# Fill-in products on TensorE in the early stage, a plan with other DMA costs, and query exponentials in two steps

## The chip, the cores and the metric

The kernel runs as one program on one core of a Trainium2 chip. A core has five engines, each with an instruction queue of its own that is worked off strictly in order: TensorE (PE in the profile, its weight loads PEld), VectorE (DVE), ScalarE (ACT), GpSimd (POOL) and SyncE (SP), which here only issues DMAs. The metric is the time of one execution in microseconds of the device; the median of three runs is given. The profile is one further execution with the hardware profiler on.

## The reference

Inputs are q, k and v of shape (8 batches, 8 heads, 576 rows, 64), three gate matrices of 512 x 768 and an output matrix of 768 x 512, the weights handed in as float64 and taken apart by the kernel.

```python
q_s = exp(q - max(q, axis=-1)); q_s /= sum(q_s, axis=-1) + 1e-9      # per row of q
k_s = exp(k - max(k, axis=2));  k_s /= sum(k_s, axis=2) + 1e-9       # per column of k, over the rows
kv = einsum('bhsd,bhse->bhde', k_s, v)
x = einsum('bhsd,bhde->bhse', q_s, kv)  -> (4608 rows, 512)
h = max(x @ w1, x @ w2, x @ w3)
out = h @ w_out
```

## The kernel before, in words

**Work.** A batch has four pairs of heads; pair n = 4b + g gives 128 of the 512 columns of x for the 576 rows of batch b. The second half of the program takes x in chunks of 512 rows (chunk c is the first 512 rows of batch c; the 64 left over from each batch make a ninth chunk). A chunk needs 18 gate products (6 column blocks j by 3 matrices), each a sum over the four pairs cc and over three matmuls per pair (high and low halves of x and w in fp32r), and then a second layer of 4 row blocks t by 6 blocks j by 3 matmuls. Each weight block (a *slice*, 24 in all: 18 of the gates, 6 of the output matrix) is loaded as float64 bits and turned into a high and a low fp32r part by ACT, DVE and POOL (`Slice.join`, `low_word`, `hi`, `lo`).

**A pair of the first two batches** (`turned`) goes through these TensorE steps: keys are transposed (`k_turned`, lines 419 and 423), their maxima taken by DVE (428 to 430), exponentials by ACT (434, 435), transposed back (442, 444), copied out (451), multiplied with v (`k_steps`, 489), scaled into a block matrix (505). The queries are shifted, exponentiated and normed (`q_steps`), transposed (`turned_steps`, 612 and 616), copied out (621, 623) and multiplied with the block matrix (`x_steps`, 639); lines 642 and 644 split the result into the two halves of x. Pairs in the list `Q_BY_ACT` have their query exponentials done as ten small ACT instructions with the row sum in each (543); the others have a subtraction on DVE or POOL (548), one ACT exponential (563) and a DVE sum (565).

**Order.** The order of all instructions on all engines is written by a planner (`Streams`) while the program is built. Each stream is a generator of `Step`s with an engine (or a choice of two), a cost in microseconds, what it waits for, which buffers ("rooms") it takes and frees, and a rank. The planner keeps a clock for each engine (S, A, V, G, T for SP, ACT, DVE, POOL, PE), lets the step begin that can begin first, and takes among those that can begin together the one of lowest rank; ranks come from due times (`AT` for the pairs of the first two batches, `FIRST + CHUNK * (b - 1)` for later batches, `SLICES_AT + SLICE * n` for slices, `GATES_AT` for gates). Instructions are emitted in the order in which the plan begins their steps, and the chip then runs each engine's queue in that order, with semaphores where data or memory demand it. The plan's costs thus decide the order only.

**Small products.** One tile named `ps` of four quarters of 128 columns (line 283) holds the small TensorE results: line 423's and 444's last transposes, 616's, the kv product of 489 and the 64-row product of 639. They take the quarters in turn (`small`, line 284). Larger results go to `pa` (attention) and `pf` (gates and second layer).

**First loads.** SP issues the loads of batch 0 and the first six slices in the order of the string `FIRST_LOADS` (a small letter is one pair's 512 rows or one slice w, a capital the 64 left-over rows). Three slices can be staged at a time (`ROOMS`).

Of the kernel before, what the change touches and what calls it, by code (L numbers as in the profile page):

```python
# [25 lines left out]
SIGNAL = 0.22  # L26
AHEAD = 0.5
DMA_LANDS = 2.0
DMA_RATE = 300.0
WAIT = 0.02  # L30

FIRST, CHUNK, SLICE = 27.0, 66.0, 2.7

AT = (7.3, 14.2, 18.2, 22.2, 39.0, 46.0, 63.0, 66.0)
STEP = (1.4, 2.8)
SLICES_AT, SLICE_STEP, SLICE_HI, SLICE_LO = 11.4, 0.18, 1.23, 1.56
GATES_AT = 50.0
FIRST_LOADS = 'kKqQvVwkqKQwvVkqwvkqvw'
ROOMS = 3, 2, 3, 4

Q_BY_ACT = (0, 1, 2, 3, 5, 6, 7)


def dve(n):
# [33 lines left out]
class Streams:  # L78
# [3 lines left out]
    def __init__(self, rooms, queued):  # L82
        self.all, self.when = [], {}
        self.queued = queued
        self.rooms = rooms
        self.taken = {}
        self.freed = {}
        self.clock = dict.fromkeys("SAVGT-", 0.0)
        self.port = 0.0
        self.queues = 0.0  # L90

# [3 lines left out]
    def ready(self, s, engine):  # L95
# [24 lines left out]
            t = max(t, self.port)  # L120
        return t

    def advance(self, s, engine=None):
        try:
            s[4] = s[0].send(engine)
        except StopIteration:
            self.all.remove(s)
# [25 lines left out]

    def issue(self, t, e, c, s):
        step = s[4]
        end = t + c
        self.clock[e] = end
        if e in step.port:
            self.port = end
        if step.kb:  # L160
            self.queues = max(self.queues, end) + step.kb / DMA_RATE
            end = self.queues + DMA_LANDS
        s[3], s[5] = end, e
        if step.gives:
            self.when[step.gives] = end
        for r, key in step.take:
            self.taken.setdefault(r, []).append(key)
        for f in step.free:
            self.freed[f] = end
        s[1] += s[2]  # L170
        self.advance(s, e)
# [3 lines left out]
def linear_attention_then_maxout_ffn(  # L175
# [26 lines left out]
    nc = tc.nc  # L202
# [75 lines left out]
    in_pf = []  # L278
    for c in range(B + 1):
        in_pf += [(c, j, i) for j in range(NJ) for i in range(3)] + [(c, "y", t) for t in range(4)]  # L280
    st = Streams({"pf": 4, "pa": 3, "ps": 4, "keT": 1, "hp": NJ, "tmp": 3, "ke": 2, "qe": 2, "qf": 1, "qt": 2, "tb": 1, "qT": 2, "qhl": 1}, {"pf": in_pf})
    late_pools, turn_pools = [], []
    quarters = ps.tile([P, 4, P], F32, name="ps")
    small = (quarters[:, i % 4, :] for i in itertools.count())

# [64 lines left out]
    class Pair:  # L352
# [19 lines left out]
        def k_load(self):  # L372
            if self.b:
                prev = self.ago("ksub") if self.n >= NP + 2 else None
                if self.turned:
                    yield Step("S", 1.1, [prev], kb=256)
                    for hh in range(2):
                        nc.sync.dma_start(out=self.kt[:, 0:4, hh, :], in_=head_rows(k, self.b, 2 * self.g + hh))
                else:
                    yield Step("S", 0.55, [prev], kb=256)  # L380
                    nc.sync.dma_start(out=self.kt[:, :, 0:4, :], in_=main_rows(k, self.b, self.hs))
                yield Step("S", 0.5, gives=("k", self.n), kb=32)
                nc.sync.dma_start(
                    out=self.kt[0:LEFT, 4] if self.turned else self.kt[0:LEFT, :, 4, :], in_=left_rows(k, self.b, self.hs)
                )

        def v_load(self):
            if self.b:
                prev = self.ago("kv") if self.n >= NP + 2 else None
                for hh in range(2):  # L390
                    yield Step("S", 0.6, [prev], kb=128)
                    nc.sync.dma_start(out=self.vt[:, hh, 0:4, 0:D], in_=head_rows(v, self.b, 2 * self.g + hh))
                yield Step("S", 0.5, gives=("v", self.n), kb=32)
                nc.sync.dma_start(out=self.vt[0:LEFT, :, 4, 0:D], in_=left_rows(v, self.b, self.hs))

        def q_load(self):
            if self.b == 0:
                return
            if self.turned:
                prev = self.ago("qsub") if self.n >= NP + 2 else None  # L400
                self.qt = qbuf[self.m]
                yield Step("S", 0.55, [prev], kb=256)
                nc.sync.dma_start(out=self.qt[:, :, 0:4, :], in_=main_rows(q, self.b, self.hs))
                yield Step("S", 0.5, gives=("q", self.n), kb=32)
                nc.sync.dma_start(out=self.qt[0:LEFT, :, 4, :], in_=left_rows(q, self.b, self.hs))
            else:
                yield Step("S", 0.55, ["turn"], gives=("q", self.n), take=[("qt", self.n)], kb=288)
                self.qt = turn_pools[0].tile([P, QS, D], F32, name="qt", bufs=2)
                nc.sync.dma_start(out=self.qt, in_=q[self.b, self.hs].rearrange("h (p s) d -> (h p) s d", s=QS))

# [108 lines left out]
        def q_steps(self):  # L519
# [6 lines left out]
            if self.turned:  # L526
# [2 lines left out]
                    out=qm.rearrange("p (h s) -> p h s", h=2), in_=src, op=ALU.max, axis=AX.X, negate=by_act  # L529
                )  # L530
                if by_act:
                    yield Step("A", rows * 0.33, take=[("qe", n)], gives=("qsub", n))
                else:
                    e = yield Step(
                        "VG", (dve(rows * D), pool(rows * D)), take=[("qe", n)], gives=("qsub", n), port="VG"
                    )
# [2 lines left out]
                sums = qs.rearrange("p (s h) -> p s h", h=2)  # L539
                if by_act:  # L540
                    for hh in range(2):
                        for s in range(5):
                            nc.scalar.activation(  # L543
                                out=qe[:, s, hh, :], in_=src[:, hh, s, :], func=AF.Exp,
                                bias=qm[:, 5 * hh + s : 5 * hh + s + 1], accum_out=sums[:, s, hh : hh + 1],
                            )
                else:
                    unit[e].tensor_tensor(
                        out=qe.rearrange("p s h d -> p h s d"),
                        in0=src,  # L550
                        in1=qm.rearrange("p (h s) -> p h s", h=2).unsqueeze(3).broadcast_to([P, 2, 5, D]),
                        op=ALU.subtract,
                    )
# [7 lines left out]
            if not by_act:  # L561
# [1 line left out]
                nc.scalar.activation(out=rows3, in_=rows3, func=AF.Exp)  # L563
                yield Step("V", dve_reduce(rows * D))
                nc.vector.tensor_reduce(out=qs, in_=rows3, op=ALU.add, axis=AX.X)
            yield Step("V", 0.28)
            nc.vector.tensor_scalar_add(out=qs, in0=qs, scalar1=1e-9)
            nc.vector.reciprocal(out=qs, in_=qs)
            which, cost = ("VG", (dve(rows * D), pool(rows * D))) if self.turned else ("V", dve(rows * D))
# [78 lines left out]
    class Chunk:  # L648
# [47 lines left out]
        def second(self, t):  # L696
# [14 lines left out]
            o = tmp.tile([P, DM], F32, name="m")  # L711
            nc.scalar.copy(out=o, in_=po)  # L712
            if c < B:
                yield Step("S", 0.5, kb=256, free=[("tmp", (c, "y", t))], rank=-1000.0)
                rows = out[c * S : c * S + CH, :]
                if c < TURNED:
                    nc.sync.dma_start(out=rows.rearrange("(p s) d -> s p d", s=4)[t], in_=o)
                else:
                    nc.sync.dma_start(out=rows[ts, :], in_=o)
            else:  # L720
                for i in range(2):
                    yield Step("S", 0.5, kb=128, free=[("tmp", (c, "y", t))] if i else (), rank=-1000.0)
                    end = (2 * t + i + 1) * S
                    nc.sync.dma_start(out=out[end - LEFT : end, :], in_=o[i * LEFT : (i + 1) * LEFT, :])

# [9 lines left out]
    def first_loads():  # L735
# [3 lines left out]
        for ch in FIRST_LOADS:  # L739
            g = seen.get(ch, 0)  # L740
            seen[ch] = g + 1
            hs = slice(2 * g, 2 * g + 2)
            low = ch.lower()
            if ch == "w":
                yield Step("S", 0.6, gives=("wst", g), kb=512, take=[("wst", g)])
                slices[g].load(start, N_ST, N_X)
            elif ch == "k":
                yield Step("S", 1.1, gives=("kmain", g), kb=256)
                for h in (2 * g, 2 * g + 1):
                    nc.sync.dma_start(out=k0[:, 0:4, h, :], in_=head_rows(k, 0, h))  # L750
            elif ch in to:
                yield Step("S", 0.55, gives=("%smain" % ch, g), kb=256)
                nc.sync.dma_start(out=to[ch][:, hs, 0:4, :], in_=main_rows(of[ch], 0, hs))
            else:
                hs = slice(2, H) if g else slice(0, 2)
                yield Step("S", 0.6, gives=(ch, g), kb=32 if g == 0 else 96)
                nc.sync.dma_start(out=to[low][0:LEFT, hs, 4, :], in_=left_rows(of[low], 0, hs))  # L757

    def landed(g):
# [32 lines left out]
        st.add(f(), 0.0)  # L792

    def slice_load(sl, late):
        yield Step("S", 0.55, ["late"] if late else (), gives=("wst", sl.n), take=[("wst2" if late else "wst", sl.n)], kb=512)
        sl.load(late_pools[0] if late else start, N_ST2 if late else N_ST, N_X2 if late else N_X)

    def slice_done(sl, late):
# [80 lines left out]
```

## Time and profile before

| what | value |
|---|---|
| median of three runs | 721.54 us (720.34 to 723.81) |
| the profiled execution, its own time | 724.52 us |
| its span, first to last instruction | 722.4 us |
| TensorE busy | 690.8 us, 96% of the span |
| VectorE busy | 404.8 us, 56% |
| ScalarE busy | 256.5 us, 36% |
| GpSimd busy | 58.4 us, 8% |
| mean granted TensorE clock | 0.993 |
| moved by DMA | 58.07 MB |

The busy time of TensorE is that of pipelined matmuls: a matmul is listed with its whole latency, and the next one begins before it has ended, so the spacing of starts and not the listed duration says how fast a group went. The chain of waits is free of this: it gives to each piece only the time that passed before the next. The shares of busy time are means over the span; the first 130 us look different from the rest, and the stages are read one by one below.

### The profile page before, as it was taken

The numbers are of one execution on the slowest core, as the hardware profiler recorded it, in microseconds if no ns is written. First come the engines' busy times: TensorE is split into PE (matmuls) and PEld (weight loads), VectorE is DVE, ScalarE is ACT, GpSimd is POOL, SyncE is SP. The second block draws the span as 40 slices with busy tenths as digits, with TensorE's granted clock in tenths as the row PEclk, the third lists the DMA queues.
The fourth block names the chain that finished last, engine by engine and source line by source line (L and its number), as shares of the span: only waits on it lengthen the run. The fifth ranks groups of instructions, "written<-read, shape, count | busy, mean of one in ns | idle before, by whom it ended". The sixth has DMA issues, their size and how long they took to land.

```text
span 722.4 us, 9841 instructions
## 1 busy us (share of the span) xinstructions
PE 690.8 (96%) x3528; PEld 553.5 (77%) x3528; DVE 404.8 (56%) x806; ACT 256.5 (36%) x610; POOL 58.4 (8%) x68
## 2 busy tenths in 40 slices
PE   3789999899999999999999999999999999999997
PEld 2557777677787887788878887888888888888886
DVE  6779997689988985675467646723222102211220
ACT  5878886333344324322342234212311111111111
POOL 2222432201000000000001000000000000000000
PEclk9989999999999999999999999999999999999999
DMA  7938414443445412530154005300100010000002
GB/s 212 257 110 252 134 61 135 141 104 99 110 125 155 113 46 69 143 109 1 33 146 126 18 25 149 83 1 10 66 1 0 15 44 0 1 33 26 1 0 59
DMA packets 86417, 58.07 MB, mean 80 GB/s; under 512 B 53344, under 2 KB 77920, under 8 KB 86368
## 3 DMA queue, kind: packets, MB, share of 16 engines
q1 hardware_dynamic: 86368, 57.44, 28.1%
q8 instruction: 28, 0.46, 0.3%
q14 instruction: 21, 0.17, 0.1%
HBM read 40.89 MB, written 9.44 MB: 70 GB/s over the span
## 4 chain that ended last, share of the span: by engine, by line
PE 85%; DVE 6%; DMA 3%; ACT 2%; SPq 2%; issue 1%; POOL 0%; DVEq 0%; ACTq 0%
PE pf L669 60%; PE pf L707 18%; PE ps L489 3%; PE pa L639 3%; ACT qe L543 1%; DMA kt<-in_k_dram 1%; PE ps L639 1%; DMA wst<-in_moe_w_dram 1%; SPq L589 1%; DVE ke L467 1%; PE pa L612 0%; DVE x L644 0%; DVE tb L576 0%; DMA qt<-in_q_dram 0%; SPq L757 0%
## 5 line engine op out<-in xcount | busy, mean ns | idle before, releaser
L669 PE MATMUL pf<-x,wh 128*128 128x512 f32 x1152 | 361.1, 395 | 1.1 <-DVE x L644 1.1
L669 PEld LDWEIGHTS pf<-x,wh 128*128 128x128 f32 x1152 | 218.0, 189 | 50.5 <-DVE x L644 1.7
L669 PE MATMUL pf<-x,wl 128*128 128x512 f32 x576 | 232.1, 403 | 0.9 <-ACT x L642 0.9
L681 DVE TENSOR_TENSOR m<-pf,m 128x512 f32<-128x512 f32 x108 | 74.3, 688 | 185.6 <-PE pf L669 185.0
L669 PEld LDWEIGHTS pf<-x,wl 128*128 128x128 f32 x576 | 109.2, 190 | 26.7 <-ACT x L642 1.1
L684 ACT CAST h_h<-m 128x512 fp32r<-128x512 f32 x54 | 33.5, 621 | 208.0 <-DVE m L681 208.0
L707 PE MATMUL pf<-ol,h_h 128*128 128x512 f32 x216 | 89.1, 412 | 0.0
L707 PE MATMUL pf<-oh,h_l 128*128 128x512 f32 x216 | 84.6, 392 | 0.0
L707 PE MATMUL pf<-oh,h_h 128*128 128x512 f32 x216 | 84.3, 390 | 0.0
L678 ACT COPY m<-pf 128x512 f32<-128x512 f32 x54 | 31.6, 586 | 52.2 <-PE pf L669 51.9
L687 DVE TENSOR_TENSOR h_l<-m,h_h 128x512 fp32r<-128x512 f32 x54 | 38.0, 704 | 20.7 <-ACT h_h L684 20.6
L707 PEld LDWEIGHTS pf<-ol,h_h 128*128 128x128 f32 x216 | 40.6, 188 | 9.0 <-issue 0.5
L707 PEld LDWEIGHTS pf<-oh,h_l 128*128 128x128 f32 x216 | 40.5, 188 | 8.9
L707 PEld LDWEIGHTS pf<-oh,h_h 128*128 128x128 f32 x216 | 40.7, 188 | 7.6 <-issue 0.5
L464 POOL PARTITION_ALL_REDUCE kma<-km x24 | 20.0, 832 | 305.3 <-DVE km L461 166.5
L669 PE MATMUL pf<-left,wh 128*128 128x512 f32 x144 | 44.3, 389 | 0.0
L712 ACT COPY m<-pf 128x512 f32<-128x512 f32 x36 | 21.1, 586 | 62.2 <-PE pf L707 61.3
L333 POOL TENSOR_TENSOR wst<-wx,wst 128x512 int32<-128x512 int32 x24 | 33.6, 1400 | 89.2 <-DVE wx L329 38.9
L576 DVE STREAM_TRANSPOSE tb<-qt 128x576 f32<-128x576 f32 x24 | 30.5, 1271 | 11.3 <-DMA qT<-tb 10.7
L669 PEld LDWEIGHTS pf<-left,wh 128*128 128x128 f32 x144 | 27.0, 188 | 5.6
L489 PEld LDWEIGHTS ps<-vt,ke 128*64 128x64 f32 (+1 forms) x560 | 18.9, 137 | 14.8 <-issue 5.0
L563 ACT ACTIVATE qt<-qt 128x576 f32<-128x576 f32 x24 | 16.5, 688 | 36.9 <-DVE qt L558 36.8
(110 smaller groups left out, 690.3 us busy)
## 6 DMA issues: line engine op xcount, KB each, us to landing
wst<-in_moe_w_dram SPq DMA_DIRECT2D x18, 512.0 KB, 4.2
out_dram<-m SPq DMA_DIRECT2D x32, 256.0 KB, 2.2
vt<-in_v_dram SPq DMA_DIRECT2D x56, 128.0 KB, 3.0
qt<-in_q_dram SPq DMA_DIRECT2D x24, 288.0 KB, 3.1
qT<-tb SPq DMA_DIRECT2D x192, 36.0 KB, 1.9
kt<-in_k_dram SPq DMA_DIRECT2D x24, 256.0 KB, 3.1
wst<-in_moe_w_out_dram SPq DMA_DIRECT2D x6, 512.0 KB, 3.3
q<-in_q_dram SPq DMA_DIRECT2D x8, 256.0 KB, 4.6
```

The lines of the kernel that those rows point to most:

```text
L333: nc.gpsimd.tensor_add(out=low.bitcast(I32), in0=x.bitcast(I32), in1=low.bitcast(I32))
L464: nc.gpsimd.partition_all_reduce(kma, km, P, bass_isa.ReduceOp.max)
L489: nc.tensor.matmul(out=kv[r, :nv], lhsT=ke[rows, s, hh, :], rhs=self.vt[rows, hh, s, 0:nv], start=(s == 0), stop=(s == 4),)
L576: nc.vector.transpose(out=tb.rearrange("p e (c s) -> p s e c", s=QS), in_=self.qt.rearrange("p s (e c) -> p s e c", e=2))
L639: nc.tensor.matmul(out=xT, lhsT=l, rhs=r[:, cs], start=(i == 0), stop=(i == last))
L669: nc.tensor.matmul(out=ps, lhsT=l[:, cc, js], rhs=r, start=(cc == 0 and t == 0), stop=(cc == NC - 1 and t == 2))
L678: nc.scalar.copy(out=m, in_=self.m.pop((j, 0)))
L681: nc.vector.tensor_max(out=m, in0=self.m.pop((j, i)), in1=m)
L684: nc.scalar.copy(out=h, in_=m)
L687: unit[e].tensor_sub(out=lo, in0=m, in1=h.bitcast(F32))
L707: nc.tensor.matmul(out=po, lhsT=l, rhs=r[:, j, :], start=(j == 0 and i == 0), stop=(j == NJ - 1 and i == 2))
L712: nc.scalar.copy(out=o, in_=po)
```

## The change

Five things are changed.

- **Fill-in products.** Before the planner emits a TensorE step it looks how long its clock for TensorE has stood. Where that is over 0.3 us and the plan's time is between 4.2 and 70 us, it first emits `int((idle - 0.3) / 0.22) + 1` products of the 128 x 128 identity with itself. Their result goes to the fourth quarter of `ps` and is never read. The plan's own clocks do not count them.
- **Small products get three quarters** in place of four, in the program and in the plan (`"ps": 3`).
- **Query exponentials.** The ten ACT instructions of line 543 are planned as two steps of five, so that the planner can put other ACT work between them; pairs 2 and 3 leave `Q_BY_ACT` and take the other way.
- **Costs of the plan.** DMA steps cost 0.64 us on SP (1.28 for two) in place of 0.5 to 0.6 (1.1), the data rate is 356 KB per us, and 0.62 of that for transfers begun before 16 us, in place of 300 throughout; loads in short rows count as larger (400 for 256 KB); the engines' clocks begin at 0.72 to 4 us and not at 0.
- **Due times** of pairs, slices and later batches are other numbers, and two of the last first loads change places.

No instruction of the computation is added or taken away except by the way that pairs 2 and 3 go.

```diff
-DMA_RATE = 300.0
+DMA_RATE, DMA_FIRST, DMA_AT_FIRST = 356.0, 0.62, 16.0
-FIRST, CHUNK, SLICE = 27.0, 66.0, 2.7
-AT = (7.3, 14.2, 18.2, 22.2, 39.0, 46.0, 63.0, 66.0)
-STEP = (1.4, 2.8)
-SLICES_AT, SLICE_STEP, SLICE_HI, SLICE_LO = 11.4, 0.18, 1.23, 1.56
+WARM_FROM, WARM_TO, WARM_IDLE, WARM_COST = 4.2, 70.0, 0.3, 0.22
+FIRST, CHUNK, SLICE = 22.7, 71.1, 2.7
+AT = (7.3, 14.2, 20.3, 22.2, 41.7, 48.7, 66.4, 62.3)
+STEP = (0.7, 3.92)
+SLICES_AT, SLICE_STEP, SLICE_HI, SLICE_LO = 11.4, 0.29, 1.44, 1.56
-FIRST_LOADS = 'kKqQvVwkqKQwvVkqwvkqvw'
+FIRST_LOADS = 'kKqQvVwkqKQwvVkqwqkvvw'
-Q_BY_ACT = (0, 1, 2, 3, 5, 6, 7)
+Q_BY_ACT = (0, 1, 5, 6, 7)
...
-        self.clock = dict.fromkeys("SAVGT-", 0.0)
+        self.clock = {"S": 0.72, "A": 2.2, "V": 4.0, "G": 3.0, "T": 0.0, "-": 0.0}
...
+    def keep_warm(self, t):
+        idle = t - max(self.clock["T"], WARM_FROM)
+        if t < WARM_TO and idle > WARM_IDLE:
+            self.fill(int((idle - WARM_IDLE) / WARM_COST) + 1)
...
     def issue(self, t, e, c, s):
         step = s[4]
+        if e == "T":
+            self.keep_warm(t)
         end = t + c
...
-            self.queues = max(self.queues, end) + step.kb / DMA_RATE
+            begun = max(self.queues, end)
+            self.queues = begun + step.kb / DMA_RATE / (DMA_FIRST if begun < DMA_AT_FIRST else 1.0)
...
-    st = Streams({"pf": 4, "pa": 3, "ps": 4, "keT": 1, "hp": NJ, "tmp": 3, "ke": 2, "qe": 2, "qf": 1, "qt": 2, "tb": 1, "qT": 2, "qhl": 1}, {"pf": in_pf})
+    st = Streams({"pf": 4, "pa": 3, "ps": 3, "keT": 1, "hp": NJ, "tmp": 3, "ke": 2, "qe": 2, "qf": 1, "qt": 2, "tb": 1, "qT": 2, "qhl": 1}, {"pf": in_pf})
+    def fill(n):
+        for _ in range(n):
+            nc.tensor.matmul(out=idle, lhsT=ident, rhs=ident, start=True, stop=True)
+    st.fill = fill
     quarters = ps.tile([P, 4, P], F32, name="ps")
-    small = (quarters[:, i % 4, :] for i in itertools.count())
+    small = (quarters[:, i % 3, :] for i in itertools.count())
+    idle = quarters[:, 3, :]
...
                 if by_act:
-                    yield Step("A", rows * 0.33, take=[("qe", n)], gives=("qsub", n))
+                    yield Step("A", 5 * 0.33, take=[("qe", n)])
...
                     for hh in range(2):
+                        if hh:
+                            yield Step("A", 5 * 0.33, gives=("qsub", n))
```

More of the change, by code (lines that the diff above doesn't have):

```diff
@@ L375, in k_load @@
                 if self.turned:
-                    yield Step("S", 1.1, [prev], kb=256)
+                    yield Step("S", 1.28, [prev], kb=400)
                     for hh in range(2):
@@ L379, in k_load @@
                 else:
-                    yield Step("S", 0.55, [prev], kb=256)
+                    yield Step("S", 0.64, [prev], kb=256)
                     nc.sync.dma_start(out=self.kt[:, :, 0:4, :], in_=main_rows(k, self.b, self.hs))
-                yield Step("S", 0.5, gives=("k", self.n), kb=32)
+                yield Step("S", 0.64, gives=("k", self.n), kb=50)
                 nc.sync.dma_start(
@@ L390, in v_load @@
                 for hh in range(2):
-                    yield Step("S", 0.6, [prev], kb=128)
+                    yield Step("S", 0.64, [prev], kb=200)
                     nc.sync.dma_start(out=self.vt[:, hh, 0:4, 0:D], in_=head_rows(v, self.b, 2 * self.g + hh))
-                yield Step("S", 0.5, gives=("v", self.n), kb=32)
+                yield Step("S", 0.64, gives=("v", self.n), kb=50)
                 nc.sync.dma_start(out=self.vt[0:LEFT, :, 4, 0:D], in_=left_rows(v, self.b, self.hs))
@@ L401, in q_load @@
                 self.qt = qbuf[self.m]
-                yield Step("S", 0.55, [prev], kb=256)
+                yield Step("S", 0.64, [prev], kb=256)
                 nc.sync.dma_start(out=self.qt[:, :, 0:4, :], in_=main_rows(q, self.b, self.hs))
-                yield Step("S", 0.5, gives=("q", self.n), kb=32)
+                yield Step("S", 0.64, gives=("q", self.n), kb=50)
                 nc.sync.dma_start(out=self.qt[0:LEFT, :, 4, :], in_=left_rows(q, self.b, self.hs))
             else:
-                yield Step("S", 0.55, ["turn"], gives=("q", self.n), take=[("qt", self.n)], kb=288)
+                yield Step("S", 0.64, ["turn"], gives=("q", self.n), take=[("qt", self.n)], kb=288)
                 self.qt = turn_pools[0].tile([P, QS, D], F32, name="qt", bufs=2)
@@ L565, in q_steps @@
                 nc.vector.tensor_reduce(out=qs, in_=rows3, op=ALU.add, axis=AX.X)
-            yield Step("V", 0.28)
+            yield Step("V", 0.34)
             nc.vector.tensor_scalar_add(out=qs, in0=qs, scalar1=1e-9)
@@ L713, in second @@
             if c < B:
-                yield Step("S", 0.5, kb=256, free=[("tmp", (c, "y", t))], rank=-1000.0)
+                yield Step("S", 0.64, kb=256, free=[("tmp", (c, "y", t))], rank=-1000.0)
                 rows = out[c * S : c * S + CH, :]
@@ L721, in second @@
                 for i in range(2):
-                    yield Step("S", 0.5, kb=128, free=[("tmp", (c, "y", t))] if i else (), rank=-1000.0)
+                    yield Step("S", 0.64, kb=128, free=[("tmp", (c, "y", t))] if i else (), rank=-1000.0)
                     end = (2 * t + i + 1) * S
@@ L744, in first_loads @@
             if ch == "w":
-                yield Step("S", 0.6, gives=("wst", g), kb=512, take=[("wst", g)])
+                yield Step("S", 0.64, gives=("wst", g), kb=512, take=[("wst", g)])
                 slices[g].load(start, N_ST, N_X)
             elif ch == "k":
-                yield Step("S", 1.1, gives=("kmain", g), kb=256)
+                yield Step("S", 1.28, gives=("kmain", g), kb=400)
                 for h in (2 * g, 2 * g + 1):
@@ L751, in first_loads @@
             elif ch in to:
-                yield Step("S", 0.55, gives=("%smain" % ch, g), kb=256)
+                yield Step("S", 0.64, gives=("%smain" % ch, g), kb=256)
                 nc.sync.dma_start(out=to[ch][:, hs, 0:4, :], in_=main_rows(of[ch], 0, hs))
@@ L755, in first_loads @@
                 hs = slice(2, H) if g else slice(0, 2)
-                yield Step("S", 0.6, gives=(ch, g), kb=32 if g == 0 else 96)
+                yield Step("S", 0.64, gives=(ch, g), kb=50 if g == 0 else 150)
                 nc.sync.dma_start(out=to[low][0:LEFT, hs, 4, :], in_=left_rows(of[low], 0, hs))
@@ L794, in slice_load @@
     def slice_load(sl, late):
-        yield Step("S", 0.55, ["late"] if late else (), gives=("wst", sl.n), take=[("wst2" if late else "wst", sl.n)], kb=512)
+        yield Step("S", 0.64, ["late"] if late else (), gives=("wst", sl.n), take=[("wst2" if late else "wst", sl.n)], kb=512)
         sl.load(late_pools[0] if late else start, N_ST2 if late else N_ST, N_X2 if late else N_X)
```

## The prediction

> **What bounds the kernel now.** I read first the page's slices of the span and the busy times by stage, then the chain of waits, then who VectorE and TensorE waited for before 62.8 us. In the page's slices (tenths of busy time, and the clock) the first two of forty show a TensorE with much idle time; in the stage rows the columns are the stretch, its length, busy us and instructions of PE, PEld, DVE, ACT and POOL, the granted clock, DMA share and GB/s.
>
> ```profile
> PE   3789999899999999999999999999999999999997
> PEclk9989999999999999999999999999999999999999
> ```
>
> ```profile
> 4.00:33.40 29.40, 17.76 (x89) 12.62 (x90) 20.16 (x48) 20.68 (x93) 6.39 (x5) 1.00 0.98 262
> ...
> 37.10:44.00 6.90, 6.02 (x32) 4.13 (x32) 5.20 (x14) 4.21 (x12) 1.29 (x1) 0.51 0.34 101
> 44.00:62.70 18.70, 16.07 (x109) 10.91 (x109) 16.71 (x36) 16.41 (x55) 5.92 (x4) 1.00 0.58 156
> 62.70:133.00 70.30, 70.25 (x362) 55.43 (x363) 59.92 (x117) 51.80 (x136) 22.20 (x22) 1.00 0.42 137
> 133.00:146.20 13.20, 9.77 (x68) 7.31 (x67) 9.86 (x20) 4.43 (x9) 1.42 (x2) 0.88 0.55 158
> ```
>
> From 62.7 to 133 us TensorE never stands (70.25 of 70.30). So an early gain counts only as far as TensorE gets more of its fixed work done before 62.7, and as VectorE keeps up behind. The clock rows say 0.51 for 37.1 to 44 and 1.00 for 4 to 33.4, but the second is not to be trusted, as the chain of waits shows (start, time until the next piece, what):
>
> ```profile
> 22.93 3.43 ACT qe L543 x20
> ...
> 28.54 1.46 PE ps L489 x20
> 30.00 2.86 PE pf L669 x6
> ...
> 37.98 1.54 PE ps L489 x20
> 39.52 2.00 PE pa L639 x2
> 41.52 1.28 PE pf L669 x3
> ...
> 43.12 0.85 PE pa L612 x4
> ...
> 62.76 19.08 PE pf L669 x83
> 81.84 0.88 PE ps L489 x20
> ...
> 87.81 0.86 PE pa L639 x2
> ...
> 95.07 0.44 PE pa L612 x4
> ```
>
> The same twenty instructions of line 489 take 1.46 us at 28.5, 1.54 at 38.0 and 0.88 at 81.8; line 639's two take 2.00 and 0.86, line 612's four 0.85 and 0.44. So TensorE ran at about half speed at 28 us too, where the clock row shows 1.00. The chain holds six cold pieces: 1.46 + 2.86 + 1.54 + 2.00 + 1.28 + 0.85 = 9.99 us. Warm they cost 0.88 + 1.38 + 0.88 + 0.86 + 0.69 + 0.44 = 5.13 (a gate matmul is 19.08 / 83 = 0.23). The half clock thus costs **4.9 us** on this chain.
>
> The other engines feel it as waits. VectorE between 5 and 46 us waited for (us in total, times, longest):
>
> ```profile
> DVE left L644 <- PE ps L444: 2.5, 1, 2.5
> ...
> DVE left L644 <- ACT left L642: 1.5, 1, 1.5
> DVE ke L451 <- ACT qe L543: 1.3, 1, 1.3
> DVE ke L451 <- PE ps L423: 0.9, 1, 0.9
> DVE qs L567 <- ACT qe L543: 0.7, 1, 0.7
> DVE km L429 <- PE ps L489: 0.4, 1, 0.4
> ```
>
> VectorE matters as much as TensorE, because the second layer of the first chunk ends with the last weight slice:
>
> ```profile
> 128.06 0.68 DVE L348 TENSOR_TENSOR ol<-wst,oh 128x512 fp32r<-128x512 f32 x1
> ```
>
> ```profile
> 133.02 0.40 PE L669 MATMUL pf<-x,wl 128*128 128x512 f32 x1
> ```
>
> The slice is split at 128.74; four row blocks of three matmuls still need it, 12 x 0.23 = 2.8 us, so the next chunk's gates could begin at 131.5 and do begin at 133.0. VectorE has only 1.5 us to spare: a gain above that must come from VectorE getting through its work sooner.
>
> **The change, part by part.** The sum is made against the profiled execution: 724.5 us, of which 722.4 are span; it lies 3.0 above the median of the runs, 721.5, to which I apply the difference.
>
> *Fill-in products and the clock.* If TensorE is at full speed from about 10 us on, TensorE's 4.9 us go, and with them VectorE's waits that hang on cold products: 2.5 + 1.5 + 0.9 + 0.4 = **-5.3** (the 1.5 is line 642, itself behind a cold product). I take VectorE's figure, since its work has the last word at 131.5. If the clock stays low it is 0.
>
> [...]
>
> How many products: TensorE idles 11.6, 0.9 and 2.6 us in the three early stage rows, 15.1 us; the plan reckons warm, so half of the 17.76 + 6.02 busy us is idle time to it as well, at most 27.0 together. At 0.22 that makes 69 to 123 products, an estimate. One costs a quarter of line 639's 512 columns: 0.86 / 4 = 0.22 warm, twice that cold.
>
> *What the products delay.* They wait for nothing of their own, but stand ahead of the next useful product. By the diff's costs the plan has the first keys at 6.26 and the first transposes at 6.98, so 12 products stand before them: 12 x 0.43 = 5.2 us at half speed, from 4.2 to 9.4, where the transposes now begin at 4.47:
>
> ```profile
> 4.47 1.08 PE L419 MATMUL pa<-ident,k 128*128 128x128 f32 x4 [4.47 <-DMA k<-in_k_dram]
> ...
> 11.37 1.12 PE L442 MATMUL pa<-ident,keT 128*128 128x128 f32 x4 [5.51 <-ACT keT L434]
> ...
> 17.00 1.53 PE L489 MATMUL ps<-v,ke 128*64 128x64 f32 x20 [0.92 <-DVE km L429]
> ```
>
> ```profile
> 7.96 0.16 DVE L430 TENSOR_TENSOR km<-km 128x1 f32<-128x1 f32 x1
> ...
> 16.73 0.21 DVE L429 TENSOR_REDUCE km<-ps 128x1 f32<-128x64 f32 x1
> ```
>
> ```profile
> 10.56 0.66 ACT L434 ACTIVATE keT<-pa,km 128x512 f32<-128x512 f32 x1
> ```
>
> The maxima are ready at 8.12 and ACT takes them at 10.56, 2.4 us later, so of the 4.9 us of delay 2.5 come through. The next idle time, 5.51 us before line 442, is filled as well, and there is a catch. Line 489's product at 17.00 goes into the first quarter of `ps`, and it was released by line 429 at 16.94, which reads the third: the quarters share one memory, and writes of TensorE wait for reads of any quarter that were emitted ahead. Products put before line 442 thus wait for line 435's read and run behind it, up to 5.5 us more for pair 0. Together 0 to 8.0; below nothing is excluded, since added products release nothing. I take a fifth, **+1.6**: four or five pairs are under way before x is complete at 62.7, and pair 0, the first of them, has its 5.51 and 2.4 us of slack in work of others that ACT and VectorE do meanwhile.
>
> *Query exponentials.* Pairs 2 and 3 leave ACT, where a pair took 3.43 us on the chain, for this way (from the row of pair 4, which goes it already):
>
> ```profile
> 56.41 0.82 DVE L548 TENSOR_TENSOR qe<-q,qm 128x640 f32<-128x640 f32 x1
> ...
> 61.29 0.81 DVE L565 TENSOR_REDUCE qs<-qe 128x10 f32<-128x640 f32 x1
> ```
>
> ```profile
> 58.42 0.74 ACT L563 ACTIVATE qe<-qe 128x640 f32<-128x640 f32 x1
> ```
>
> ```profile
> L322 DVE TENSOR_SCALAR wx<-wst 128x512 uint32<-128x512 uint32 x7 | 2.9, 413 | 2.6 <-DMA wst<-in_moe_w_dram 2.6
> ```
>
> VectorE gains work, 2 x (0.82 + 0.81) = 3.3 us (1.6 if both subtractions go to POOL), and loses the waits on line 543, 1.3 + 0.7 = 2.0. ACT is freed of 2 x (3.43 - 0.74) = 5.4 us and can take back slices' line 322, which the plan gives to either engine: four of the seven, 1.7 us, is my choice between none and 2.9. Net 3.3 - 2.0 - 1.7 = **-0.4**, from -3.3 (POOL takes the subtractions, ACT all seven) to +3.3 (nothing saved). The step split in two adds no instruction.
>
> *Three quarters, other costs, other due times.* Three quarters can make a product wait that finds a free one now. The waits of TensorE before 62.8:
>
> ```profile
> PE pa L442 <- ACT keT L434: 9.0, 2, 5.5
> ...
> PE ps L489 <- ACT qf L623: 2.8, 1, 2.8
> PE ps L489 <- DVE km L429: 1.1, 2, 0.9
> ```
>
> The 2.8 is a product that found its quarter taken, so the price of a fourth less is 0 to another 2.8; since any read of `ps` holds up TensorE already, I take 0. The new order of loads and due times is bounded by what is left of VectorE's idle time, the same rows: from -2.0 to +2.0, taken as 0, hidden behind the 70.25 busy us of TensorE. That cover is gone if a slice comes over 1.5 us late.
>
> **Sum:** -5.3 + 1.6 - 0.4 = -4.1: the profiled execution would be 720.4, the median 721.5 - 4.1 = **717.4 us**. Half a per cent, 3.6 us, is about what a measurement of this kernel can tell from no change.
>
> **The rivals.**
>
> *The products stand behind reads (slower).* Of TensorE's waits above, 9.0 + 2.8 + 1.1 = 12.9 us end with an engine that reads `ps`. If each is followed by products of its own length, the clock's gain is eaten: -5.7 for clock and exponentials, +2.5 for the first block, plus a share of 12.9. From a quarter of it on (3.2) the change is slower than before; at three quarters it is +6.5, 728.0. For it: line 489 released by line 429 above. Against it: most of the 9.0 lies before 23 us, where other pairs' work is at hand.
>
> [...]
>
> *Nothing comes through.* x is complete earlier, but slice 23 is not, because VectorE's 3.3 us of new work and the late start (1.6) eat the waits saved; or the clock does not stay up because TensorE still stands while products wait for reads, and the change does not do what it says. -5.3 - 2.0 + 3.3 + 1.6 = -2.4 with nothing taken over by ACT, +1.6 with no clock gain and the exponentials even; about 721.
>
> *More than the sum.* The stage from 133 to 146.2 loses 13.2 - 9.77 = 3.4 us of TensorE's time, and at clock 0.88 another 1.2. It hangs on the order in which the first pairs of batch 2 come; a new order may close it: 717.4 - 4.6 = 712.8.
>
> **How the numbers follow.** Forecast 0.36 (own range 714 to 719, five parts in six of it faster by over 3.6), nothing comes through 0.28 (719 to 723), products behind reads 0.22 (above 725), more than the sum 0.14 (below 714). Faster: 0.30 + 0.14 = 0.44; within half a per cent: 0.06 + 0.28 = 0.34; slower: 0.22. From 711 to 726 some 0.17 is left out, half of the slow case and half of the best one.
>
> **What would show it.** Right: line 489's twenty instructions take 0.9 us from the second pair on; line 419 begins near 9 us; VectorE's waits on line 444 and on line 642 are gone; x's last line 644 ends some us before 62.7, and the last split of `ol` before 126. The slow rival shows as groups of identity products that begin right at the end of lines 429, 435, 451 or 623, with the useful product behind them. The second shows as an early x with the last split of `ol` still near 128. The prediction is wrong if TensorE's transposes still take 0.85 us after 15 us, or if TensorE stands for long after 62 us.

## The result

| kernel | median us | ratio to the kernel before, same chip (95% interval) |
|---|---|---|
| before | 722.35 | |
| changed | 743.12 | 1.0291 (1.027 to 1.0312) |

The change makes the kernel 2.9% slower, some 20.8 us. The profiled execution went from 724.52 to 742.59 us, its span from 722.4 to 740.8. That lies outside the range of the prediction.

### The profile page after: what moved, and what is told of

The parts are those of the page before. It is cut to its first block, busy times and chain, and to the rows that moved or that the text cites. A ratio compares the mean times of both kernels' runs of the same rounds, so it can differ in the third digit from the quotient of the medians.

```text
span 740.8 us, 10184 instructions
## 1 busy us (share of the span) xinstructions
PE 707.8 (96%) x3708; PEld 573.1 (77%) x3708; DVE 403.4 (54%) x801; ACT 253.7 (34%) x574; POOL 65.0 (9%) x75
## 4 chain that ended last, share of the span: by engine, by line
PE 85%; DVE 4%; issue 4%; ACT 2%; SPq 2%; DMA 1%; POOL 1%; ACTq 0%; DVEq 0%; POOLq 0%
PE pf L689 53%; PE pf L727 20%; PE ps L297 4%; PE pa L659 3%; PE ps L507 3%; SPq L609 1%; PE ps L659 1%; DMA kt<-in_k_dram 1%; DVE tb L596 1%; PE pa L632 0%; ACT qe L563 0%; PE pa L460 0%; POOL kma L482 0%; DVE m L701 0%; POOL h_l L707 0%
## 5 line engine op out<-in xcount | busy, mean ns | idle before, releaser
L707 DVE TENSOR_TENSOR h_l<-m,h_h 128x512 fp32r<-128x512 f32 x48 | 33.7, 702 | 20.6 <-ACT h_h L704 20.6
L297 PE MATMUL ps<-ident 128*128 128x128 f32 x180 | 26.6, 303 | 18.0 <-ACT keT L453 4.5
L482 POOL PARTITION_ALL_REDUCE kma<-km x24 | 17.7, 738 | 280.2 <-DVE km L479 140.8
L297 PEld LDWEIGHTS ps<-ident 128*128 128x128 f32 x180 | 23.6, 209 | 21.0 <-ACT keT L453 5.6
L485 DVE TENSOR_TENSOR ke<-kt,kma 128x640 f32<-128x640 f32 x24 | 19.5, 814 | 24.8 <-POOL kma L482 24.8
```

The costliest lines, as they stand in the source:

```text
L297: nc.tensor.matmul(out=idle, lhsT=ident, rhs=ident, start=True, stop=True)
L707: unit[e].tensor_sub(out=lo, in0=m, in1=h.bitcast(F32))
```

## The profile after

The first of the page's slices shows a TensorE that is busier than before (6 tenths for 3), the second does not (6 for 7):

```profile
PE   6688999989999999999999799999999999999997
...
PEclk9989999999999999999999999999999999999999
```

The stage rows (columns as in the prediction) are cut at 75.2, 148 and 160 us where those of before are cut at 62.7, 133 and 146.2: TensorE is steadily busy from 75.5 us on, not from 62.8.

```profile
4.00:30.00 26.00, 20.01 (x162) 18.32 (x163) 11.15 (x26) 12.91 (x57) 5.03 (x4) 1.00 0.96 264
30.00:75.20 45.20, 36.95 (x250) 28.27 (x249) 32.08 (x77) 28.23 (x82) 8.57 (x7) 0.89 0.36 103
75.20:148.00 72.80, 71.26 (x369) 55.83 (x368) 61.41 (x119) 51.79 (x135) 23.51 (x22) 1.00 0.43 135
148.00:160.00 12.00, 9.40 (x67) 7.16 (x66) 7.02 (x15) 4.92 (x9) 1.42 (x2) 0.86 0.47 143
160.00:740.80 580.80, 570.23 (x2868) 463.57 (x2864) 288.90 (x552) 154.34 (x289) 24.31 (x28) 1.00 0.22 60
```

VectorE and ACT tell the story of the first row: they work 11.15 and 12.91 of the first 26 us, where before they were busy 20.16 and 20.68 of 29.4. TensorE's busy time is largely that of the products. In the chain of waits they are pieces of their own (start, us, what):

```profile
4.01 4.31 PE ps L297 x24
8.31 0.45 PE pa L437 x4
...
11.03 3.17 PE ps L297 x26
14.20 0.45 PE pa L460 x4
...
15.61 1.83 PE ps L297 x14
17.44 0.90 PE ps L507 x20
...
37.90 2.56 PE pf L689 x6
40.46 0.78 PE pa L632 x4
...
72.88 2.05 PE ps L297 x16
...
75.47 24.52 PE pf L689 x108
```

At first the clock does what was hoped for: line 437's four transposes take 0.45 us at 8.3 us (0.85 for such a group at 43 before) and line 507's twenty instructions 0.90 at 17.4 (1.46 at 28.5 before). It does not stay up: six gate products of line 689 take 2.56 us at 37.9, where six took 1.38 at full speed before, and the granted clock of the stretch from 30 to 40 us is 0.71. And 3.17 us of products stand between the end of what line 460 waited for and line 460. The page's group of the products, and who TensorE waited for before 100 us:

```profile
L297 PE MATMUL ps<-ident 128*128 128x128 f32 x180 | 26.6, 303 | 18.0 <-ACT keT L453 4.5 <-DVE ident L268 4.0 <-ACT qf L643 2.5
```

```profile
PE ps L297 <- ACT keT L453: 4.5, 2, 2.5
PE ps L297 <- DVE ident L268: 4.0, 1, 4.0
PE ps L297 <- ACT qf L643: 2.5, 3, 1.5
PE ps L297 <- DVE left L664: 2.1, 2, 1.5
PE ps L297 <- ACT ke L469: 2.1, 1, 2.1
PE ps L297 <- DVE km L447: 1.1, 2, 0.7
PE ps L297 <- DVE ke L469: 0.9, 1, 0.9
PE ps L297 <- ACT bdf L523: 0.8, 1, 0.8
```

There are 180 instructions, two to a product, so 90 products, 26.6 us. Of the 18.0 us of waiting in front of them, 4.0 are for the identity itself; the other 14.0 are all for engines that read `ps` (lines 453, 643, 664, 469, 447, 523). The products read nothing but the identity and write a quarter that nobody reads; still they waited for reads of the other quarters, 14.0 us in all, and then ran in full in front of the product that the read had made ready. It goes the other way too: line 523, which reads the keys' product out of `ps`, waited twice, 2.8 us in all, for products that stood behind that one:

```profile
ACT bdf L523 <- PE ps L297: 2.8, 2, 2.2
```

The last split of batch 0's 512 rows of x, and the last split of the output weights (the low part `ol` of the last slice):

```profile
71.08 0.68 DVE L664 TENSOR_TENSOR x<-pa,x 128x512 fp32r<-128x512 f32 x1
```

```profile
144.55 0.68 DVE L366 TENSOR_TENSOR ol<-wst,oh 128x512 fp32r<-128x512 f32 x1
```

Below, x is called complete when these 512 rows are: at 71.8 us here, 62.7 before. The steady stage of TensorE begins at 75.5 for 62.8 us, 12.7 later, and the last split comes at 144.55 for 128.06, 16.5 later. A third loss lies far behind all this. From 160 us on TensorE idles 580.8 - 570.2 = 10.6 us (7.0 in the answering stage before), most of it at one place, which the instructions of POOL and TensorE show:

```profile
412.49 1.61 POOL L707 TENSOR_TENSOR h_l<-m,h_h 128x512 fp32r<-128x512 f32 x1 [7.09 <-DVE qm L576]
420.39 0.72 POOL L482 PARTITION_ALL_REDUCE kma<-km  x1 [6.30 <-issue]
```

```profile
423.74 0.80 PE L689 MATMUL pf<-x,wl 128*128 128x512 f32 x1 [5.46 <-DVE m L701]
```

The new plan gives 6 of the 54 low halves of the hidden layer (`h_l`, line 707) to POOL, where VectorE did all 54 before. The five all-reduces that come right after one begin 5.9 to 6.3 us after its end, this one 6.30, with nothing that the profile shows to wait for; VectorE, in order, stands 6.78 us for this one, and TensorE 5.46 us behind VectorE.

## The experiments

In their expectations theory A is that the products wait for reads of `ps` and push useful products back, B that the new plan is itself worse, C that the products cost TensorE's time wherever they go, D that a warm TensorE is worth nothing.

**The changed kernel without its products.**

```diff
         if t < WARM_TO and idle > WARM_IDLE:
-            self.fill(int((idle - WARM_IDLE) / WARM_COST) + 1)
+            pass
```

> The changed kernel without its 90 identity products; all else of the change stays (three quarters, new costs and due times, query exponentials). Theory A (the products wait for reads of ps and push the useful products back): x of batch 0 is complete about 12.7 us earlier, near 63 us, and the time falls from 743.1 to about 730. Theory B (the new plan is itself worse, the products cost nothing): the time stays above 738.

Measured 725.9 us, 1.0021 of the kernel before (0.9999 to 1.0042). B falls: by the two ratios 2.70 of the 2.91%, 19.5 of the 21 us, are the products'. In the profiled execution x is complete at 53.9 us, 8.8 before the old kernel, which is more than A expected; yet the time is no better than before, since the last split comes at 124.67 (3.4 earlier) and the late all-reduces remain, with one wait of TensorE of 4.9 us.

**The same with the products in a bank that nothing reads.** A bank here means the place of one tile of 128 x 512 numbers that TensorE writes, such as `ps` with its four quarters or one tile of `pf`. A tile of `pf` is taken ahead of the gates and written until the fourth gate needs its bank.

```diff
+    spare = pf.tile([P, CH], F32, name="pf")
     def fill(n):
-        for _ in range(n):
-            nc.tensor.matmul(out=idle, lhsT=ident, rhs=ident, start=True, stop=True)
+        if len(st.taken.get("pf", ())) < 4:
+            for _ in range(n):
+                nc.tensor.matmul(out=spare[:, 0:P], lhsT=ident, rhs=ident, start=True, stop=True)
```

> The changed kernel with its products written to a bank of pf that nothing reads, and only until the fourth gate takes that bank; nothing then makes them wait for reads of ps. Theory A: no product waits for ACT or VectorE, TensorE is warm from about 8 us, and the time lies below that of the kernel without products by up to the 4.9 us of the half clock: 725 to 730. A rival C (products cost as TensorE time alone, wherever they are written): as slow as the changed kernel, 740 to 743. Theory B: 738 or more, whatever bank.

727.0 us, 1.0053 (1.0032 to 1.0073). As A has it, it is far below 743. But it isn't below the kernel without products.

**The kernel before with the rule for products,** in `ps` with three quarters:

> The kernel before with the rule for products and three quarters only; costs, due times and exponentials are the old ones. Theory A: x is complete later by about as much as in the changed kernel, 730 to 735. Theory B: 722, within 3.

752.5 us, 1.0397 (1.0366 to 1.0428): 28 us slower than before, over twice what A expected. Its blocks are longer: 54 instructions stand before the first product of the keys' exponentials, 26 in the changed kernel. This run does not separate the lost quarter from the products.

**The kernel before, its order untouched, products in the spare bank:**

> The kernel before, its order untouched and four quarters, with the products written to a bank of pf that nothing reads, until the fourth gate takes it. Theory A: the clock's gain of my sum without its cost, 717 to 720. Rival D (a warm TensorE is worth nothing, since VectorE and ACT have the last word): 722, within 1.5. Rival C: 730 or more.

720.2 us, 0.9957 (0.9935 to 0.998), 3.1 us by the ratio. That is the clock, less what the products delay, in the old order: the first pair's kv product takes 0.95 us at 17.6, where it took 1.53 at 17.0 before, x is complete at 59.9 for 62.7, the last split comes 1.9 earlier. D and C fall; the gain is there, less than the 5.3 of the sum.

**The low half on VectorE alone, no products.**

```diff
-            e = yield Step("VG", (0.61, 1.28), gives=("h", c, j), free=[("tmp", (c, j))], port="VG")
+            e = yield Step("V", 0.61, gives=("h", c, j), free=[("tmp", (c, j))], port="V")
```

> The changed kernel without products, and the low half of the hidden layer only on VectorE, as all 54 of them were before (the changed plan gives 6 to POOL). Theory P (an all-reduce on POOL that follows such an elementwise POOL instruction starts some 6 us late, and TensorE once stands 4.9 us for it): 725.9 falls by about 5, to 718 to 722, and no wait of TensorE above 2 us is left after 150 us. Rival Q (that wait moves elsewhere, since VectorE has the last word): 724 or more.

719.9 us, 0.9948 (0.9928 to 0.9968). Only the first all-reduce, at 135.64, is still late (5.81 us, 5.82 before), and after 150 us no wait of TensorE above 2 us is left. P holds: by the two ratios the six POOL instructions cost 0.73%, 5.3 us.

**The changed kernel with only that edit:**

> The changed kernel with its products in ps, the low half only on VectorE. If the two causes add, 743.1 falls by about 5, to 737 to 739; if the late all-reduces were covered by the products' delay, it stays at 742 to 744.

736.7 us, 1.0191 (1.0176 to 1.0206), 1.0% or 7 us below the changed kernel: the two causes add, within the noise (0.73% without products).

**The bank alone.** Two kernels with the low half on VectorE and the same 72 products at the same places of the order (the traces show the same order on TensorE, VectorE and ACT throughout), none after the fourth gate's start; one writes them to `ps`, the other to the spare bank.

> The changed kernel with the low half on VectorE and its products in ps, but none after the fourth gate's first product: the same products at the same places as the next run, which writes them to the spare bank. Theory A (reads of ps hold the products up): x of batch 0 complete at 65 us or later, 728 to 735. Rival C (what counts is TensorE's time for them): x at 58 us and within 2 us of the next run.

> The changed kernel with the low half on VectorE and all its products until the fourth gate in the spare bank of pf. The pair to the run before. From the earlier run of this without the change to the low half: x at 58 us; time 5 us below its 727.0, 720 to 723. Theory A: 6 us or more below the run before. Rival C: the same as it within 2 us.

733.7 us, 1.0146 (1.0112 to 1.018), and 720.7 us, 0.9966 (0.9948 to 0.9985): **13.0 us** for the place of a result that nobody reads. TensorE in `ps`:

```profile
11.99 4.80 PE L297 MATMUL ps<-ident 128*128 128x128 f32 x26 [2.08 <-ACT keT L453]
16.63 0.60 PE L460 MATMUL pa<-ident,keT 128*128 128x128 f32 x4
...
18.20 1.83 PE L297 MATMUL ps<-ident 128*128 128x128 f32 x14 [0.87 <-DVE ke L469]
```

and in the spare bank:

```profile
10.28 3.17 PE L300 MATMUL pf<-ident 128*128 128x128 f32 x26
13.29 0.60 PE L462 MATMUL pa<-ident,keT 128*128 128x128 f32 x4
...
13.83 1.73 PE L300 MATMUL pf<-ident 128*128 128x128 f32 x14
```

The same 26 instructions begin when TensorE is free, at 10.28, without the 2.08 us for line 453's read, and the transposes follow at 13.29 for 16.63. Half of these 3.3 us is the later start; the other half is the block itself, 4.80 us for 3.17, its instructions 0.18 us apart for 0.12. In the changed kernel's trace the same block took 3.17 too, so it is this execution that was slower; that its clock was low again for part of the block is read from the spacing alone. x is complete at 58.2 for 72.7. In `ps` the products waited 11.5 us in all for reads, without the 4.0 for the identity. As a bank is here also one tile of the program, no run tells whether it is the tile or the bank that sets these waits.

**Half as many products,** from 6.5 us of the plan, in the spare bank, low half on VectorE:

```diff
-WARM_FROM, WARM_TO, WARM_IDLE, WARM_COST = 4.2, 70.0, 0.3, 0.22
+WARM_FROM, WARM_TO, WARM_IDLE, WARM_COST = 6.5, 70.0, 0.3, 0.44
```

> As the kernel without products and with the low half on VectorE, plus products in the spare bank of pf, half as many for a given idle time and only from 6.5 us of the plan on. Theory A2 (products delay only where they are more than the real idle time): x of batch 0 complete at 53 to 55 us, TensorE at full speed by 15 us, time within 2 us of the kernel without products. Rival C2 (every product in front of a useful one delays it): x some 2 us later and the time 2 us longer.

716.5 us, 0.9917 (0.9891 to 0.9942): faster than both kernels; 0.31% or 2.2 us by the ratios below the one without products, with intervals that overlap, so that this difference is not shown. From the early stage of TensorE and VectorE and the last split:

```profile
11.44 0.95 PE L509 MATMUL ps<-v,ke 128*64 128x64 f32 x20
```

```profile
53.68 0.68 DVE L666 TENSOR_TENSOR x<-pa,x 128x512 fp32r<-128x512 f32 x1
...
124.98 0.68 DVE L368 TENSOR_TENSOR ol<-wst,oh 128x512 fp32r<-128x512 f32 x1
```

With 34 products TensorE is at full speed at 11.4 us: line 509's twenty instructions take 0.95 us, where without products the same group took 1.53 at 9.7. With the 72 in the spare bank above, x comes 3.8 us later (58.2 for 54.4) and the time is 0.49% longer, with intervals that do not meet: here products that waited for no read still delayed what followed them, where there were more than the real idle time holds.

**The same with the fourth quarter given back to `ps`:**

> Half the products in the spare bank from 6.5 us, low half on VectorE (716.5 before), and ps with its four quarters again, in the program and in the plan. If the fourth quarter was missed, 712 to 715; if any read of ps holds up TensorE whatever the quarter, as in the trace of before, within 1.5 us of 716.5.

717.6 us, 0.9928 (0.9905 to 0.9951): no difference that can be told. x is complete 3.9 us sooner, and the last split comes later all the same:

```profile
49.75 0.68 DVE L666 TENSOR_TENSOR x<-pa,x 128x512 fp32r<-128x512 f32 x1
...
127.32 0.68 DVE L368 TENSOR_TENSOR ol<-wst,oh 128x512 fp32r<-128x512 f32 x1
```

```profile
PE pf L691 <- DVE wl L368: 6.8, 4, 4.3
```

TensorE now waits 6.8 us for split weights (0.7 with three quarters). Up to the last split VectorE has the last word, as the prediction read it. Behind it the order of the plan counts: here TensorE is busy for all of the 25 us after that split, at a granted clock of 1.00, where before it was busy 21.57 of 25 at 0.93; the span ends 586.3 us after that split, 593.7 before.

**The old list for the query exponentials,** no products, low half on VectorE:

> As the kernel without products and with the low half on VectorE, but pairs 2 and 3 do their query exponentials in the old way on ACT. If the exponentials are what makes x complete 8.8 us earlier in the new plan, x comes 3 to 7 us later here and the time is 1 to 4 us longer; if it is the costs and due times, x and time stay within 1.5 us.

724.1 us, 1.0016 (0.9995 to 1.0037), against 0.9948 with the new list: the new way of pairs 2 and 3, with the order that the plan makes of it, is worth 0.68%, 4.9 us by the ratios, a little more than the 1 to 4 expected. x is complete at 60.1 us, 57.9 with the new list. Part of it goes with the clock: the executions with the old list had a mean granted clock of 0.984 to 0.987, those with the new list 0.987 to 0.996; at 0.986 and 0.987 the old list took 723.1 and 723.2 us, at 0.987 the new one 720.4 to 721.6. With the old list TensorE stands behind ACT:

```profile
PE ps L636 <- ACT keT L453: 6.5, 2, 5.0
```

## Why the prediction was wrong

The likeliest case and its range failed; the slow rival named the mechanism and was given 0.22 and too small a price. By steps, with differences of the ratios to the kernel before (1% is 7.2 us):

- **What bounds the kernel** held up to the last split, which VectorE sets: without products 8.8 us of x became 3.4 us at the last split, and with four quarters 3.9 us of x became a last split that came 2.3 us later. What follows the last split is not fixed, though: with four quarters the kernel was 0.72% faster than before with a last split only 0.7 us earlier, since TensorE lost nothing in the next 25 us. That is the stage that the rival "more than the sum" named; it was right about it, if not about the whole.
- **The clock** was right as a mechanism (full speed from 8.3 us after the change, by 11.4 with half the products; that it would come from about 10 us on was the author's estimate, which no row of before shows), though in the changed kernel it fell again between 30 and 41 us (0.71 for 30 to 40), and oversized: -5.3 in the sum, -3.1 in the old order and -2.2, not clear of noise, in the new one (the run with half the products against the one without).
- **What the products delay** is the step that failed. With the clock's gain the sum had -3.7 us for the products; taking them out of the changed kernel gained 2.70%, 19.5 us. For their delay the sum took +1.6, a fifth of the bounds, because pair 0's delay would be covered by other pairs' work. Two things were wrong in it. It counted only the two blocks of pair 0, where the plan fills such idle times up to 70 us: the chain still holds 2.05 us of products at 72.9. And it took waits and products as if the one could hide the other, where 12 of the 15 blocks began at the end of a read of `ps` and then ran in full. The bank alone cost 13.0 us, and the products after the fourth gate some 0.45%, 3 us (1.0191 for 1.0146, intervals that just touch).
- **The number of products,** 69 to 123, held: 90 (its 15.1 us of idle time leave out another 1.9 between 33.4 and 37.1, which would not have changed this). The first transposes were forecast near 9 us and came at 8.15: the first block took 4.31 us and not 5.2, since its instructions begin 0.21 us apart up to 6.9 us and 0.11 from there on. The 2.5 us that this was to cost pair 0's keys did not come: they were exponentiated at 9.90, and 10.56 before. It was the products behind that read that put the next transposes at 14.04 for 11.37.
- **Query exponentials,** -0.4, were undersized: about -4.9 with the order that the plan makes of it. The sum charged VectorE for the new work and saw as ACT's gain only waits of VectorE; that ACT, freed of 5.4 us, releases TensorE earlier (6.5 us of waits for line 453 with the old list) was left out.
- **Other costs and due times,** taken as 0 within 2.0 and called covered, hid the third loss: the new plan moved six low halves to POOL, at 5 to 7 us (whether costs, due times or the new query list did it, no run separates). The trace of before showed the price once, as the 5.51 us that VectorE stood for the first all-reduce, and the prediction did not ask what would repeat it.
- **Three quarters** at 0: agrees with 716.5 and 717.6 us.
- **The slow rival** said +6.5 at three quarters of its 12.9 us. The products' waits for reads summed to 14.0 us, near that figure, and it was not a share of it that counted: in the two runs that differ in the bank alone, 11.5 us of such waits went with 13.0 us of time. A likely reason, not tested by itself, is that all engines run in the plan's order and a late TensorE step holds VectorE and ACT up too (VectorE was busy 11.15 of the first 26 us).

The account from before to after, in per cent of the ratio: new plan and exponentials without products -0.52, 72 products in a free bank +0.18, the same in `ps` +1.80, the later products +0.45, the low halves on POOL +1.00, together +2.91. The second is within its uncertainty. What the due times and the DMA costs are worth apart from each other no run separates.

## What to carry to other kernels

Work that is meant to fill idle time is free only if it neither waits for anything nor is longer than the time that really is idle; ask of a filler what its memory is shared with, because a result that nobody reads still waited here 14.0 us for readers of its bank, and a reader of that bank 2.8 us for it. A plan's idle time is not the chip's: filled to the brim, the plan loses the slack that takes up its errors (72 products in the spare bank took 0.49% longer than 34), and half the filling was enough for full speed at 11.4 us. Look at the engine that has a choice of work after each change of a plan's numbers; six instructions moved to another engine cost as much as the change was to bring.

## What was not expected of the hardware

- The all-reduce on POOL began 5.7 to 6.5 us after an elementwise POOL instruction right before it, with no wait shown, and not only the first time (5.82 before, 5.68 to 6.30 after the change, 5.75 to 6.45 without products); between two all-reduces the shortest pause was 2.02 us. It goes the other way too: the six elementwise low halves of the changed kernel began 6.8 to 7.3 us after the all-reduce before them, two of them, at 477.15 and 492.31, with nothing shown to wait for. In the run with four quarters the first all-reduce began some 0.2 us after its input (line 481 ended at 135.35, line 487 waited 0.98 us from there for the all-reduce, and one takes some 0.7): there any such time passed behind another wait. No run here shows what the time is spent on.
- The moment from which TensorE runs at full speed differs between executions and matters. The runs without products with the low half on either engine have the same order of instructions on TensorE throughout, and on VectorE in the first 130 us, and yet (each time first the run with POOL allowed, then the one without):

```profile
23.57 0.95 PE L507 MATMUL ps<-v,ke 128*64 128x64 f32 x20 [0.32 <-DVE km L447]
```

```profile
24.18 1.53 PE L507 MATMUL ps<-v,ke 128*64 128x64 f32 x20 [0.32 <-DVE km L447]
```

```profile
53.21 0.69 DVE L664 TENSOR_TENSOR x<-pa,x 128x512 fp32r<-128x512 f32 x1
```

```profile
57.20 0.69 DVE L664 TENSOR_TENSOR x<-pa,x 128x512 fp32r<-128x512 f32 x1 [1.33 <-ACT x L662]
```

  One execution is at full speed for the second group of line 507 (0.95 us), the other is not (1.53), and x is 4.0 us apart. In the executions of such kernels the times spread by 5 us (722.6 to 727.6 and 716.4 to 721.6). In the second kernel three executions with a mean granted clock of 0.994 to 0.996 took 716.4 to 716.6 us, five with 0.987 took 720.4 to 721.6. So a moment read off one execution, as those of x here, can be off by some us.
- The row of the granted clock shows 1.00 for TensorE in the first 30 us before and after the change, also where a group takes 1.6 times as long (line 489 of the kernel before: 1.53 us at 17.0 and 28.5, 0.95 at 47.7); there the speed shows in the spacing of instructions and not in the row.
